# A list scheduler, token-major hash bits and DMA transposes in a masked attention with a maxout feed-forward on one core

## The chip, the cores and the metric

The kernel runs on one core of a Trainium2 chip. The metric is the device time in microseconds (us) of one execution. A run of a kernel is several executions, and its median is quoted with the lowest and the highest. An execution counts as slow when it is more than 1.5% above the fastest of the same kernel in that run; verdicts use the fast ones alone. Names of engines in profile lines: PE is TensorE's matmuls, PEld its weight loads, DVE VectorE, ACT ScalarE, POOL GpSimd, SP the engine whose queue issues most of the DMAs. "SPq" is SP's queue, "PEclk" the share of its full clock that TensorE was granted.

## The reference, cut to what matters

```python
# 4 batches, 8 heads, 768 tokens, 64 dims, 6 hash bits
q_bits = (einsum('bhsd,dk->bhsk', q, proj) > 0)       # same for k
mask   = bucket(q)[..., :, None] == bucket(k)[..., None, :]
scores = where(mask, q @ k.T / sqrt(64), -1e9)
attn   = exp(scores - max); attn = attn / (sum(attn) + 1e-9)
x      = heads side by side of (attn @ v)             # 3072 x 512
h      = maximum(maximum(x @ w1, x @ w2), x @ w3)     # 512 -> 768, three times
out    = h @ w_out                                    # 768 -> 512
```

## The kernel before

Each q and k is split into an fp16 value and its fp16 residual, side by side in 128 columns, and turned so that these 128 lie on the partitions. The hash needs all 128 rows. After it, six bit rows take the place of the first six residual rows, scaled so that a pair of different buckets gets an exponent far below zero. A score is then a matmul of 64 + 6 = 70 rows, and no mask is ever applied.

The work comes in 192 *units* (batch, half of the queries, pair of heads, head, a third of the keys). Each unit is a pair of score matmuls, one exponential over 128 x 768 on ScalarE, and six attend matmuls:

```python
def score(u):
    ...
    for i in range(2):
        nc.tensor.matmul(sc[:, i, 0:HQ], kT[0:KR, hh * NCH + 2 * j + i, :],
                         qT[0:KR, hh * NCH + hf * CH : hh * NCH + (hf + 1) * CH, :], ...)
    nc.scalar.activation(AT[:], sc[:, :, 0:HQ], ActFn.Exp, bias=bias_t[:], scale=EXP_SCALE)
```

The hash is bit-major: 32-column weights, then a comparison, then the bits are written into rows 64 to 69 of the turned operand by VectorE, or by eight small DMAs in batch 1:

```python
def hash_half(b, pr, half):
    ...
    hash_cmp(hbs[b, pr][:, half * HQ : (half + 1) * HQ], hash_mm([g]))
def hash_head_rows(b, pr, hh):
    for i, n in enumerate("qk"):
        dst = T[n, b, pr][D : D + NBITS, ...]
        hash_row(dst, hbs[b, pr][o : o + NBITS, :])
```

The normalised x is turned by TensorE before the feed-forward. The order is by hand: work is hung on unit numbers, and the feed-forward's groups of matmuls (18 of the first layer and 3 of the second for each half batch) are rationed by a credit:

```python
front(0, 1, 2); at(3, lambda: load_pair(0, 3, nc.sync)); ...
for u in range(N + LAG + 4):
    if u < N: score(u)
    if LAG <= u < N + LAG and not late: attend(u - LAG)
    for pe, fn in todo.pop(u, []): fn()
    if u >= begin:
        credit += rate
        while atoms and credit >= atoms[0][0] / 2: ...
```

The softmax here doesn't subtract the row's maximum and nothing guards it: scores larger than these inputs give would overflow.

Of the kernel before, what the change touches and what calls it, by code (L numbers as in the profile page):

```python
# [8 lines left out]
FP32 = mybir.dt.float32  # L10
# [3 lines left out]


@with_exitstack
def kernel(
# [24 lines left out]
    KR = D + NBITS  # L42

# [5 lines left out]

    konst = ctx.enter_context(tc.tile_pool(name="konst", bufs=1))  # L50
    raw = ctx.enter_context(tc.tile_pool(name="raw", bufs=4))
    spl = ctx.enter_context(tc.tile_pool(name="spl", bufs=3))
    opnd = ctx.enter_context(tc.tile_pool(name="opnd", bufs=8))
    vpool = ctx.enter_context(tc.tile_pool(name="vpool", bufs=2))
    atp = ctx.enter_context(tc.tile_pool(name="atp", bufs=4))
    small = ctx.enter_context(tc.tile_pool(name="small", bufs=4))
    xp = ctx.enter_context(tc.tile_pool(name="xp", bufs=3))
    hp = ctx.enter_context(tc.tile_pool(name="hp", bufs=12))
    op = ctx.enter_context(tc.tile_pool(name="op", bufs=4))
# [5 lines left out]


    raws = {}

    def raw_tile(n, b, pr):
        if (n, b, pr) not in raws:  # L70
            raws[n, b, pr] = raw.tile([P, 2, NCH * D], FP32, tag=n + "32", name=n + "32")
        return raws[n, b, pr]

    def load(n, b, pr, eng, heads=(0, 2)):
        h0, h1 = heads
        r_ = raw_tile(n, b, pr)
        src = {"q": q, "k": k, "v": v}[n][b, 2 * pr + h0 : 2 * pr + h1]
        eng.dma_start(r_[:, h0:h1, :], src.rearrange("h (p c) d -> p h (c d)", c=NCH))
# [3 lines left out]
    load("q", 0, 0, nc.sync, (0, 1))  # L82
    load("k", 0, 0, nc.sync, (0, 1))
    load("q", 0, 0, nc.sync, (1, 2))
    load("k", 0, 0, nc.sync, (1, 2))
    load("v", 0, 0, nc.sync)
    for n in "qkv":
        load(n, 0, 1, nc.sync)

    bias_t = konst.tile([P, 1], FP32, name="bias_t")  # L90
    nc.vector.memset(bias_t[:], EXP_BIAS)
    warm = konst.tile([P, 1], FP32, name="warm")
    nc.scalar.activation(warm[:], bias_t[:], ActFn.Exp)
    iden = konst.tile([P, P], FP16, name="iden")
    make_identity(nc, iden[:])
    ones = konst.tile([P, P], FP16, name="ones")
    nc.vector.memset(ones[:], 1.0)
    vones = []
    for i in range(2):
        t = konst.tile([P, H, NCH, D + 2], FP16, name=f"vone{i}", tag=f"vone{i}")  # L100
        nc.vector.memset(t[:, :, :, D : D + 1], 1.0)
        vones.append(t)

    ph = konst.tile([D, NBITS], FP16, name="ph")
    pr32 = konst.tile([D, NBITS], FP32, name="pr32")
    PA, PB = [], []
    for i in range(2):
        for n, l in (("PA", PA), ("PB", PB)):
            l.append(konst.tile([P, 32], FP16, name=f"{n}{i}", tag=f"{n}{i}"))
            nc.vector.memset(l[i][:], 0.0)  # L110

    def make_p(i):

        if i == 0:
            nc.vector.tensor_copy(ph[:], p32[:])
            nc.vector.tensor_tensor(out=pr32[:], in0=p32[:], in1=ph[:], op=AluOp.subtract)
        for o in (0, D):
            for l, src in ((PA, ph), (PB, pr32)):
                nc.vector.tensor_scalar(out=l[i][o : o + D, NBITS * i : NBITS * (i + 1)], in0=src[:],
                                        scalar1=1024.0, scalar2=None, op0=AluOp.mult)  # L120

    w_sb = [konst.tile([P, NJ, DF], FP16, name=f"w{i}_sb") for i in range(3)]
    wout_sb = konst.tile([P, NF, DM], FP16, name="wout_sb")

    def load_w(i, half):
        w_ap = (moe_w1, moe_w2, moe_w3)[i].rearrange("(c p) f -> p c f", p=P)
        f = slice(half * DF // 2, (half + 1) * DF // 2)
        nc.gpsimd.dma_start(w_sb[i][:, :, f], w_ap[:, :, f])


    T = {}
    S16 = {}

    def operands(b, pr):
        for n in "qk":
            S16[n, b, pr] = spl.tile([P, 2 * NCH, 2 * D], FP16, tag=n + "s", name=n + "s")
            T[n, b, pr] = opnd.tile([P, 2 * NCH, P], FP16, tag=n + "T", name=n + "T")

    def split_h(n, b, pr, eng, heads=(0, 2)):
        a = slice(heads[0] * NCH, heads[1] * NCH)  # L140
        x32 = raws[n, b, pr][:].rearrange("p h (c d) -> p (h c) d", d=D)[:, a, :]
        o = S16[n, b, pr][:, a, 0:D]
        if eng is nc.scalar:
            nc.scalar.activation(o, x32, ActFn.Copy, scale=QS)
        else:
            eng.tensor_scalar(out=o, in0=x32, scalar1=QS, scalar2=None, op0=AluOp.mult)  # L146

    def split_r(n, b, pr, heads=(0, 2)):
        a = slice(heads[0] * NCH, heads[1] * NCH)
        x32 = raws[n, b, pr][:].rearrange("p h (c d) -> p (h c) d", d=D)[:, a, :]  # L150
        s = S16[n, b, pr]
        nc.vector.scalar_tensor_tensor(out=s[:, a, D : 2 * D], in0=x32, scalar=QS,  # L152
                                       in1=s[:, a, 0:D], op0=AluOp.mult, op1=AluOp.subtract)

    def xbar(n, b, pr):
        nc.sync.dma_start_transpose(T[n, b, pr][:], S16[n, b, pr][:].rearrange("p a d -> p (a d)"))

    def pe_T(n, b, pr, hh):
        ps = mm_ps.tile([P, 512], FP32, tag="mm", name="tps")
        p16 = ps[:].bitcast(FP16)  # L160
        for c in range(NCH):
            nc.tensor.transpose(p16[:, c * P : (c + 1) * P], S16[n, b, pr][:, hh * NCH + c, :], iden[:])  # L162
        return p16

    def evac_T(p16, n, b, pr, hh, eng, c0=0, c1=NCH):
        o = T[n, b, pr][:, hh * NCH + c0 : hh * NCH + c1, :].rearrange("p a t -> p (a t)")
        if eng is nc.scalar:
            nc.scalar.copy(o, p16[:, c0 * P : c1 * P])
        else:
            nc.vector.tensor_copy(o, p16[:, c0 * P : c1 * P])  # L170

    def hash_mm(sets):

        hps = mm_ps.tile([P, 512], FP32, tag="mm", name="hps")
        ws = [(i, l[i]) for l in (PA, PB) for i in range(len(sets))]
        for m, (i, w) in enumerate(ws):
            for g, (t, hh, half) in enumerate(sets[i]):
                a = hh * NCH + half * CH
                nc.tensor.matmul(hps[32 * g : 32 * (g + 1), 0:HQ], w[:], t[:, a : a + CH, :],  # L179
                                 start=m == 0, stop=m == len(ws) - 1)  # L180
        return hps

    def hash_cmp(out, hps):
        nc.vector.tensor_scalar(out=out, in0=hps[:, 0:HQ], scalar1=0.0, scalar2=0.5,  # L184
                                op0=AluOp.is_gt, op1=AluOp.subtract)

    def hash_row(dst, src):
        nc.vector.tensor_scalar(out=dst, in0=src, scalar1=2 * BIT, scalar2=None, op0=AluOp.mult)  # L188

    hbs = {}  # L190

    def hash_pair(b, pr):
        hb = small.tile([P, HQ], FP16, tag="hb", name="hb")
        hbs[b, pr] = hb
        g = [(T[n, b, pr], hh) for hh in range(2) for n in "qk"]
        hash_cmp(hb[:], hash_mm([[(t, hh, half) for t, hh in g] for half in range(2)]))
        hash_row(hb[:], hb[:])

    def hash_half(b, pr, half):
        if half == 0:  # L200
            hbs[b, pr] = small.tile([P, S], FP16, tag="hb2", name="hb2")
        g = [(T[n, b, pr], hh, half) for hh in range(2) for n in "qk"]
        hash_cmp(hbs[b, pr][:, half * HQ : (half + 1) * HQ], hash_mm([g]))

    def hash_head_rows(b, pr, hh):
        for i, n in enumerate("qk"):
            dst = T[n, b, pr][D : D + NBITS, hh * NCH : (hh + 1) * NCH, :].rearrange("p a t -> p (a t)")
            o = 32 * (2 * hh + i)
            hash_row(dst, hbs[b, pr][o : o + NBITS, :])

    def hash_rows(b, pr):
        hb = hbs.pop((b, pr))
        for g, (n, hh) in enumerate((("q", 0), ("k", 0), ("q", 1), ("k", 1))):
            for half in range(2):
                a = hh * NCH + half * CH
                o = 32 * g + NBITS * half
                nc.sync.dma_start(T[n, b, pr][D : D + NBITS, a : a + CH, :].rearrange("p a t -> p (a t)"),
                                  hb[o : o + NBITS, :])

    def hash_head(b, pr, hh):  # L220

        tq, tk = T["q", b, pr], T["k", b, pr]
        hb = small.tile([P, HQ], FP16, tag="hb", name="hb")
        hash_cmp(hb[:], hash_mm([[(tk, hh, 0), (tq, hh, 0), (tk, hh, 1), (tq, hh, 1)]]))
        for g, (t, half) in enumerate(((tk, 0), (tq, 0), (tk, 1), (tq, 1))):
            a = hh * NCH + half * CH
            hash_row(t[D : D + NBITS, a : a + CH, :].rearrange("p a t -> p (a t)"),
                     hb[32 * g : 32 * g + NBITS, :])
# [290 lines left out]
```

## Time and profile before

| | before |
|---|---|
| time, median of 3 runs | 308.07 us (307.59 to 308.14) |
| span of the profiled execution, mean granted clock | 306.0 us, 0.974 |
| TensorE's own work, by the prediction's prices | 258 us |
| span less that work | 48 us |
| an exponential: duration, start to start | 0.90 us, 0.79 us |

The span runs from the first to the last instruction. A busy TensorE isn't one at its peak, since records of matmuls overlap (a score matmul's record lasts 332 ns in the mean, and a pair of them takes 0.33 us from start to start); the prediction explains its prices. The rows in the page's part 2 are a digit or character for each fortieth of the span (7.65 us), in tenths.

### The profile page before, as it was taken

To read this page: it belongs to the slowest core of one execution; us is meant where nothing else is said; L and a number is where in the kernel's file an instruction comes from. 1 tells how busy PE (TensorE), PEld (TensorE's weight loads), DVE (VectorE), ACT (ScalarE), POOL (GpSimd) and SP (SyncE) were. 2 spreads that over 40 slices of the span, in tenths; PEclk is the share of its full clock that TensorE was granted. 3 is DMA by queue.
4 is the path that set the end of the run, shared out by engine and by line. 5 is a ranking of instruction groups with operands and counts; after the bars stand their busy time and mean duration, and the time that the engine had idled before them with its cause. 6 is when DMAs were issued, how large, how long until landed. Compare 5 with 4: busy or idle time off the path is not lost.

```text
span 306.0 us, 7090 instructions
## 1 busy us (share of the span) xinstructions
PE 276.1 (90%) x2896; PEld 176.6 (58%) x2896; DVE 212.0 (69%) x455; ACT 200.6 (66%) x265; POOL 9.3 (3%) x17
## 2 busy tenths in 40 slices
PE   3847888989969989999999989999999999999994
PEld 1444565656646656565666556656666665666551
DVE  5687996877995867969587677969664454455551
ACT  3425658968646667777778676868676787786220
POOL 1370000000000000000000000000000000000000
PEclk9969979999997999999999999999999999999998
DMA  7999940006326285915809490926002001100202
GB/s 216 372 287 264 227 131 2 3 5 185 132 56 172 45 233 130 222 39 113 249 15 230 114 246 20 237 95 136 2 1 105 2 0 54 53 1 2 103 0 104
DMA packets 46080, 35.20 MB, mean 115 GB/s; under 512 B 26656, under 2 KB 42976, under 8 KB 46048
## 3 DMA queue, kind: packets, MB, share of 16 engines
q1 hardware_dynamic: 42016, 31.61, 37.7%
q0 software_dynamic: 3952, 3.15, 6.5%
q8 instruction: 22, 0.36, 0.5%
q14 instruction: 10, 0.08, 0.1%
q10 hardware_dynamic: 80, 0.00, 0.0%
HBM read 25.17 MB, written 6.29 MB: 103 GB/s over the span
## 4 chain that ended last, share of the span: by engine, by line
PE 74%; DVE 18%; ACT 3%; issue 2%; DMA 1%; SPq 0%; DVEq 0%; ACTq 0%
PE ps L329 28%; PE sc L265 16%; PE av L285 9%; PE po L341 9%; PE hps L179 4%; PE tps L162 4%; DVE qs L152 3%; ACT AT L269 2%; DVE hb L184 2%; DVE ks L146 2%; DVE ks L152 2%; PE xps L315 2%; DVE kT L188 2%; PE svp L244 1%; DVE t L301 1%
## 5 line engine op out<-in xcount | busy, mean ns | idle before, releaser
L269 ACT ACTIVATE AT<-sc,bias_t 128x768 f16<-128x768 f32 x192 | 169.1, 902 | 73.2 <-PE sc L265 72.7
L329 PE MATMUL ps<-xT,w_sb 128*128 128x384 f16 x576 | 112.4, 327 | 1.9 <-DVE ht L336 1.7
L265 PE MATMUL sc<-qT,kT 70*128 70x384 f16 x384 | 96.4, 332 | 4.2 <-ACT AT L269 1.6
L285 PEld LDWEIGHTS <-AT 128*128 128x128 f16 x1152 | 61.3, 98 | 31.1 <-issue 6.9
L336 DVE TENSOR_TENSOR ht<-ht,ps 128x384 f16<-128x384 f16 x96 | 52.9, 552 | 34.4 <-PE ps L329 31.6
L285 PE MATMUL av<-vone,AT 128*128 128x65 f16 x1152 | 67.1, 193 | 4.4 <-DVE t L301 4.3
L329 PEld LDWEIGHTS <-w_sb 128*128 128x128 f16 x576 | 50.8, 98 | 30.9 <-issue 5.8
L265 PEld LDWEIGHTS <-kT 70*128 70x128 f16 x384 | 34.0, 100 | 23.9 <-issue 6.4
L341 PE MATMUL po<-wout_sb,ht 128*128 128x512 f16 x144 | 34.8, 379 | 0.0
L334 ACT CAST ht<-ps 128x384 f16<-128x384 f32 x48 | 22.8, 474 | 16.3 <-PE ps L329 16.1
L301 DVE TENSOR_TENSOR t<-av,mv 128x390 f32<-128x390 f32 x32 | 17.9, 560 | 10.1 <-PE av L285 10.0
L184 DVE TENSOR_SCALAR hb<-hps 128x384 f16<-128x384 f32 x28 | 15.2, 553 | 8.7 <-PE hps L179 8.6
L162 PE MATMUL tps<-iden,qs 128*128 128x128 f16 x96 | 9.7, 259 | 12.7 <-DVE qs L152 11.9
L341 PEld LDWEIGHTS <-ht 128*128 128x128 f16 x144 | 12.8, 97 | 13.1 <-issue 0.6
L347 DVE COPY osb<-po 128x512 f32<-128x512 f32 x16 | 11.0, 688 | 11.5 <-PE po L341 11.5
L305 DVE TENSOR_TENSOR xn<-t,rr 128x384 f16<-128x384 f32 x32 | 17.9, 558 | 1.1
L152 DVE SCALAR_TENSOR_TENSOR qs<-q,qs 128x768 f16<-128x768 f32 (+1 forms) x17 | 16.5, 972 | 0.1
L162 PEld LDWEIGHTS <-qs 128*128 128x128 f16 x96 | 7.4, 116 | 14.7 <-DVE qs L152 13.3
L316 DVE COPY xT<-xps 128x384 f16<-128x384 f16 x32 | 11.3, 353 | 6.2 <-PE xps L315 5.9
L152 DVE SCALAR_TENSOR_TENSOR ks<-k,ks 128x768 f16<-128x768 f32 (+1 forms) x17 | 15.3, 906 | 0.3
L179 PE MATMUL hps<-kT,PA 128*32 128x384 f16 x64 | 11.1, 343 | 1.0 <-DVE kT L170 0.9
L170 DVE COPY kT<-tps 128x768 f16<-128x768 f16 x16 | 8.6, 553 | 4.3 <-PE tps L162 4.2
(43 smaller groups left out, 172.9 us busy)
## 6 DMA issues: line engine op xcount, KB each, us to landing
v<-in_v_dram SPq DMA_DIRECT2D x16, 384.0 KB
out_dram<-osb SPq DMA_DIRECT2D x24, 256.0 KB
q<-in_q_dram SPq DMA_DIRECT2D x15, 384.0 KB
k<-in_k_dram SPq DMA_DIRECT2D x15, 384.0 KB
w_sb<-in_moe_w_dram POOLq DMA_DIRECT2D x6, 384.0 KB, 13.3
wout_sb<-in_moe_w_out_dram POOLq DMA_DIRECT2D x1, 768.0 KB, 22.0
q<-in_q_dram SPq DMA_DIRECT2D x2, 192.0 KB
k<-in_k_dram SPq DMA_DIRECT2D x2, 192.0 KB
```

Of the source, the lines that this page charges most:

```text
L152: nc.vector.scalar_tensor_tensor(out=s[:, a, D : 2 * D], in0=x32, scalar=QS, in1=s[:, a, 0:D], op0=AluOp.mult, op1=AluOp.subtract)
L162: nc.tensor.transpose(p16[:, c * P : (c + 1) * P], S16[n, b, pr][:, hh * NCH + c, :], iden[:])
L179: nc.tensor.matmul(hps[32 * g : 32 * (g + 1), 0:HQ], w[:], t[:, a : a + CH, :], start=m == 0, stop=m == len(ws) - 1)
L184: nc.vector.tensor_scalar(out=out, in0=hps[:, 0:HQ], scalar1=0.0, scalar2=0.5, op0=AluOp.is_gt, op1=AluOp.subtract)
L265: nc.tensor.matmul(sc[:, i, 0:HQ], kT[0:KR, hh * NCH + 2 * j + i, :], qT[0:KR, hh * NCH + hf * CH : hh * NCH + (hf + 1) * CH, :], start=Tr ...
L269: nc.scalar.activation(AT[:], sc[:, :, 0:HQ], ActFn.Exp, bias=bias_t[:], scale=EXP_SCALE)
L285: nc.tensor.matmul(av[:, o : o + D + 1], AT[:, i, c * P : (c + 1) * P], vones[b % 2][:, 2 * pr + hh, 2 * j + i, 0 : D + 1], start=first, s ...
L301: nc.vector.tensor_tensor(out=t[:, :, :, 0 : D + 1], in0=av[:, :, :, 0 : D + 1], in1=mvs[b, pr][:].unsqueeze(2).to_broadcast([P, 2, CH, D ...
L329: nc.tensor.matmul(ps[:, 0:HQ], w_sb[i][:, jc, fb * P : (fb + 1) * P], xT[:, jc, :], start=jc == 0, stop=jc == NJ - 1)
L334: nc.scalar.copy(ht[:], ps[:, 0:HQ])
L336: nc.vector.tensor_tensor(out=hts[fb][:], in0=hts[fb][:], in1=ps[:, 0:HQ], op=AluOp.max)
L341: nc.tensor.matmul(ps[:], hts[fb][:, c * P : (c + 1) * P], wout_sb[:, fb, :], start=fb == 0, stop=fb == NF - 1)
```

## The change

The intent is to take work from TensorE and VectorE (transposes to DMA, the means' additions to GpSimd, a cheaper hash) and to let a program order all the engines' instructions from estimated durations, so that TensorE is filled earlier. The diff has 1,028 lines. Its core:

```diff
-    at(u + LAG + 3, lambda: x_T(b, hf, pr), 0.2)
-    ... all at(), at_end(), front(), tail(), prep() and the credit loop
+class Plan:
+    LAT = {"PE": 0.22, "DVE": 0.1, "ACT": 0.1, "POOL": 0.1, "SP": 2.0, "POOLQ": 2.0}
+    def run(self):     # greedy: each free engine takes the ready task of least priority number
+        ...
+                    if t.xfer:
+                        dma = max(dma, now + dur) + t.xfer
+                        end = dma + self.LAT[e]
# hash: a chunk of tokens is the weights, 12 columns are streamed
-                nc.tensor.matmul(hps[32 * g : 32 * (g + 1), 0:HQ], w[:], t[:, a : a + CH, :], ...)
+                    nc.tensor.matmul(hps[:, a * 2 * NBITS : (a + 1) * 2 * NBITS], T[b, pr][:, a, :], PAB[:], ...)
+        nc.vector.tensor_tensor(out=bv, in0=hv[:, :, sl, 0:NBITS], in1=neg[:, :, sl, :], op=AluOp.is_gt)
# bits: turned by TensorE, written to DRAM, read back as rows 64 to 69
+            nc.tensor.transpose(p16[0:R, n * P : (n + 1) * P], bit[:, n, :, :].rearrange(...), iden[:])
+        nc.sync.dma_start(drs[b, pr][:].rearrange("n r t -> r n t"), bts.pop((b, pr))[:])
+        nc.sync.dma_start(T[b, pr][D : D + NBITS, :, :].rearrange(...), drs.pop((b, pr))[:].rearrange(...))
# (only batch 0 pair 0 is turned a second time by TensorE, bits included, head by head)
-    blocks = [(0, hf, pr) for pr, hf in ((0, 0), (0, 1), (1, 0), ...)]
+    blocks = [(0, 0, ((0, 0), (1, 0))), (0, 0, ((0, 1), (1, 1)))]      # head 0 of both halves first
# q, k of batches 1 to 3 (of 2 and 3 already before) and x of six of the eight half batches
+        nc.sync.dma_start_transpose(operand(b, pr)[:, a0:a1, :], S16[b, pr][:, a0:a1, :]...)
+        nc.sync.dma_start_transpose(x_tile(b, hf)[:, pr, :]..., xn[:]...)
-        nc.scalar.activation(AT[:], sc[:, :, 0:HQ], ActFn.Exp, bias=bias_t[:], scale=EXP_SCALE)
+        nc.scalar.activation(AT[:], scs.pop(u)[:, :, 0:HQ], ActFn.Exp, bias=EXP_BIAS, scale=EXP_SCALE)
```

## The prediction

> **What bounds the kernel now.** I read the page's busy lines first, then stretches of time, then the groups, then the timeline and the chain at both ends. The page says that TensorE is nearly full:
>
> ```profile
> PE 276.1 (90%) x2896; PEld 176.6 (58%) x2896; DVE 212.0 (69%) x455; ACT 200.6 (66%) x265; POOL 9.3 (3%) x17
> ...
> PE   3847888989969989999999989999999999999994
> ```
>
> But busy is not dense, since matmuls overlap. So I priced each block of matmuls by the distance from its start to the start of the next block in the timeline and the chain. A score pair is 0.33 us (150.25 to 150.58), six attend matmuls 0.18 (153.54 to 153.72), four first-layer matmuls 0.65 (1.30 for eight), six second-layer ones 1.30 (3.90 for 18), one pair's hash 0.87 (16 matmuls), twelve transposes 0.67, that is 0.056 each. A 130-column mean matmul I take as a transpose too. TensorE's own work is then 192 x 0.33 = 63.4, 192 x 0.18 = 34.6, 144 x 0.65 = 93.6, 24 x 1.30 = 31.2, 16 x 0.87 = 13.9, 192 + 96 + 96 small ones x 0.056 = 21.5: **258 us**. The span is 306, so **48 us are lost**. The same prices on the instruction counts of each stretch say where: 17 us before 24 us, 5 up to 40, 14 between 40 and 100, about 6 in all between 100 and 290, 4.5 at the end. The stretches (columns: PE, PEld, DVE, ACT, POOL busy, granted clock, DMA share, GB/s):
>
> ```profile
> 16.00:24.00 8.00, 4.30 (x38) 3.63 (x39) 6.72 (x9) 1.34 (x2) 5.06 (x7) 0.57 1.21 276
> ...
> 40.00:60.00 20.00, 17.52 (x226) 12.70 (x226) 15.81 (x35) 15.26 (x19) 0.00 (x0) 0.91 0.09 28
> ...
> 150.00:200.00 50.00, 48.94 (x512) 30.58 (x511) 38.65 (x81) 36.51 (x50) 0.00 (x0) 1.00 0.66 145
> 200.00:250.00 50.00, 50.00 (x513) 31.17 (x510) 30.63 (x67) 38.03 (x51) 0.00 (x0) 1.00 0.17 49
> ```
>
> From 100 us on TensorE sets the pace and there is little left. Before that something else does: the fixed order feeds scores late, so ScalarE waits, and the feed-forward work that could fill TensorE doesn't exist until 66.9 us. In the timeline:
>
> ```profile
> 17.56 2.09 DVE L152 SCALAR_TENSOR_TENSOR qs<-q,qs 128x768 f16<-128x768 f32 x1
> ...
> 21.90 0.90 ACT L269 ACTIVATE AT<-sc,bias_t 128x768 f16<-128x768 f32 x1 [5.47 <-PE sc L265]
> ```
> ```profile
> 37.39 4.06 ACT L269 ACTIVATE AT<-sc,bias_t 128x768 f16<-128x768 f32 x5 [0.73 <-PE sc L265]
> ```
>
> VectorE reaches pair 1's split only at 16.2 us, and ScalarE starves 5.5 us. The last line gives the true price of an exponential: (4.06 - 0.90) / 4 = 0.79 us from start to start. The end is pure TensorE, then a copy and a store until 306:
>
> ```profile
> 286.24 11.37 PE ps L329 x69
> 297.62 3.90 PE po L341 x18
> 301.54 0.69 DVE osb L347
> ```
>
> [...] The first q load here is issued at 0.74 and used at 3.30[...]. [...] The split above took 2.09 us against a mean of 1.03 while GpSimd cast v and issued weights[...].
>
> **The change part by part.**
>
> *Token-major hash.* Per pair, 16 matmuls (0.87) become 24 of 12 columns, each with its own weights. By the attend rate of 0.03 each that is 0.72 (estimate), plus two bit transposes, 0.11. Over 16 pairs this is even within 1 us. VectorE loses comparison and rows (2 x 0.55 + 4 x 0.35 = 2.5 per pair) for three small operations and a copy, about 1.1 (estimate). But for every pair except batch 0's first the bits go through DRAM, two dependent DMAs.
>
> *Transposes.* Batch 1's q and k leave TensorE (96 transposes), batch 0 pair 0 gets 24 more for its second pass: 192 to 120, -4.0 us. x goes by DMA in 24 of 32 blocks (batch 0's second half too): 96 to 24, -4.0. Means: 96 matmuls to 24 + 12, -3.4, with 36 additions of v moved to GpSimd. With the hash, TensorE's work falls from 258 to about **246 us**, -12. The 32 warm-up matmuls lie in idle time.
>
> *Order.* I read it from the built program. After unit 12 TensorE holds pair 3's hash and bits before unit 13's score, and on the DMA queue the read of pair 1's bits stands behind two bit writes, the three loads of batch 1's first pair, and an x transpose which needs the norm after unit 12. Feed-forward starts near unit 36, after a 30-unit half block instead of 36. After unit 192, 72 first-layer groups and 12 second-layer groups remain, against 17 or so and 3 now.
>
> The path:
> 1. *Start to unit 13.* The inputs land no earlier, and the first scores now need bits, then a second transpose and copy, and stand behind six to eight splits and copies of 0.5 to 0.8 us on ScalarE: first exponential near 13.5 us against 9.6. Twelve exponentials (9.5) with four more copies or splits (3): unit 12 near 26. Then norm 1.9, the x transpose's issue 1.4, two bit issues 1.3, 2 us landing, while the loads (1.15 MB beside weights, some 130 GB/s, 9 us) run ahead of the bits in the same queue. So unit 13 at about **35 us**, against 31.0 now.
> 2. *Units 13 to 48*, ScalarE-bound: 36 x 0.79, seven casts or splits at 0.82 - 0.10, one copy 0.4: **34 us**, to 69.
> 3. *Units 49 to 192.* TensorE's prices on its order give 137 us, ScalarE's on its own 131. With the greater taken for each twelve units, **138**, to 207. With two score buffers and both engines 95% full I add 6% of phases 2 and 3, **10** (now 100 to 290 us loses 3% with ScalarE at three quarters). To 217.
> 4. *Tail*: 72 x 0.65 + 12 x 1.30 + 0.6 = **63**, to 280. The three evacuations per 1.95 us fit (VectorE 1.1, ScalarE 0.5).
> 5. *Last copy and store*: **4.5**. Span 284.5. The measured time exceeds the span by 2.1 now, so 286.6. [...] I round to **285**, 7.5% less.
>
> So of 23 us, 12 are work removed and 11 are idle time that the earlier filling removes, nearly all between 40 and 100 us.
>
> **Rivals.**
> *The scheduler's plan holds*: no waiting behind loads, unit 13 at 28 us, friction 3%: 285 - 7 - 5 = 273. For it: TensorE's order is dense; against: it plans 0.73 for an exponential, 0.79 here, and DMA contention isn't in it.
> *ScalarE or VectorE becomes the bound*: in-order queues arranged for durations 5 to 12% too short make each engine wait for the other. 12% friction and another 3 us at the start: 298. For it: ScalarE at 131 of 138 and VectorE near 10 of 12 us per twelve units; against: the tail of 63 us can't suffer.
> *The one DMA queue becomes the bound*: 24 transposes of q and k (1.4 to 3.3 us of issue now), 24 of x, 30 bit DMAs, in order. I count some 19 us of issue where 37 are available before unit 49, so it is hidden; if heads of the queue stall for each pair, 300 to 310.
>
> **Range and chances.** 80%: 274 to 297, from the first rival to nearly the second. Faster by over 2% means under 301.9: 0.93. Within 2%: 0.05. Slower: 0.02.
>
> **What would show it.** Right: 2,882 matmuls (2,256 of scores, attend and feed-forward, 384 hash, 30 bits, 120 + 24 transposes, 36 means, 32 warm-up); first exponential after 12 us; a hole in ScalarE between 26 and 36 us; feed-forward from about 60 us; exponentials close to 0.79 apart afterwards; about 63 us without exponentials at the end, dense. Wrong: scores waiting on bit reads at pairs of batches 1 to 3, an exponential waiting more than 1 us repeatedly after unit 48, first-layer matmuls waiting for x, or holes in the tail.

The sum comes to 284.5 us of span, and to 286.6 with the 2.1 us by which the time of before exceeds its span.

## More of the kernel before

```profile
PEclk9969979999997999999999999999999999999998
DMA  7999940006326285915809490926002001100202
DMA packets 46080, 35.20 MB, mean 115 GB/s; under 512 B 26656, under 2 KB 42976, under 8 KB 46048
```

The granted clock stays near full (0.974 in the mean) but for short dips (0.50 from about 17 to 24, 41 to 44 and 92 to 96 us), and the DMA engines are idle from about 46 to 69 us and in shorter stretches later.

## The result, and the profile after

| | time | fast executions |
|---|---|---|
| before, same session | 308.11 us (307.59 to 310.41, 4 runs) | |
| after | 294.0 us (291.31 to 298.56, 4 runs) | ratio 0.9495, 95% interval 0.9435 to 0.9556 |

Ratios are the mean time of one kernel's fast executions over that of the other's in the same rounds, so not quite the ratio of the medians. The change is 5% faster: inside the predicted range, 9 us above the predicted value.

The profile taken with this result fell on the slow execution (298.56 us, clock 0.918; the three fast ones had 0.934 to 0.942). Its page:

```profile
span 296.7 us, 7201 instructions
...
PE 270.2 (91%) x2882; PEld 178.0 (60%) x2882; DVE 178.6 (60%) x399; ACT 202.8 (68%) x291; POOL 34.3 (12%) x53
...
PE   7789149999999988997979999999999999999994
...
PEclk9699755557999999999979999999999999999999
DMA  7999999968889999999976101121001102020202
...
DMA packets 70835, 41.68 MB, mean 140 GB/s; under 512 B 51422, under 2 KB 67550, under 8 KB 70802
```

There is a hole in PE at the fifth and sixth digit (30 to 44 us), and the clock is at half from about 33 to 70 us (0.50 in every window of 1 us). Nothing like either is in the page of before. The DMA engines are busy for six tenths of the time or more in every slice up to about 160 us.

To have a fast trace, the same kernel was run again (e0 below: span 292.6 us). It shows the same two things, and it is the one read from here on. First its windows (columns as in the prediction: PE, PEld, DVE, ACT, POOL busy, granted clock, DMA share, GB/s):

```profile
28.00:40.00 12.00, 3.08 (x61) 2.44 (x59) 6.83 (x16) 4.83 (x7) 1.08 (x1) 0.75 1.22 237
40.00:60.00 20.00, 18.80 (x162) 11.95 (x163) 10.45 (x25) 14.92 (x19) 5.00 (x9) 0.50 1.09 250
...
160.00:230.00 70.00, 70.00 (x788) 46.37 (x787) 35.80 (x77) 59.38 (x82) 0.00 (x0) 1.00 0.13 38
```

The hole's cause is in the chain of waits (start, duration, what):

```profile
32.66 0.32 PE bps L298 x2
33.00 0.38 ACT bt L168
33.40 0.33 SPq L307
33.83 6.95 DMA T<-dr
40.83 0.84 PE sc L353 x2
41.75 0.82 ACT AT L359
...
44.82 0.64 PE sc L353 x2
45.46 0.33 PE av L371 x6
```

The read (`T<-dr`) is that of pair 1's bits. It takes 6.95 us, and unit 13's score can't start before it lands. The three lines before it are not pair 1's: those bits were turned at 21.92 us, and their write was issued at 23.02. What is turned (L298), copied and written (L307) from 32.66 us on are pair 3's bits. The chain passes through them because pair 1's read stands behind that write in SP's queue. Behind the hole a score pair takes 0.64 us and six attend matmuls 0.33, against 0.33 and 0.18 at full clock: the pace is 0.97 us a unit, and TensorE sets it. SP's queue shows what stands before the read:

```profile
28.67 0.31 SPq L307 DMA_DIRECT2D dr<-bt  x1
29.07 0.40 SPq L216 DMA_DIRECT2D q<-in_q_dram  x1
29.57 0.41 SPq L216 DMA_DIRECT2D k<-in_k_dram  x1
30.07 0.42 SPq L216 DMA_DIRECT2D v<-in_v_dram  x1
31.16 1.28 SPq L413 DMA_TRANSPOSE xT<-xn  x1
33.40 0.33 SPq L307 DMA_DIRECT2D dr<-bt  x1
33.83 1.70 SPq L310 DMA_DIRECT2D T<-dr  x2
```

Three loads of 384 KB and a transpose were issued in the five microseconds before it, and the DMA share is above 1. The trace also has the time at which each DMA landed. Pair 1's write had landed by 29.3 us, 4.5 us before its read was issued. The three loads landed at 36.4, 37.7 and 38.8 us, and the last of the weights, from GpSimd's queue, at 37.0. The read isn't slow by itself: the same reads of later pairs, issued at 157.93 and 162.61 us with a DMA share of 0.24 (157 to 165 us), landed in 2.2 us. How much of the 6.95 us is due to the loads and how much to the weights was not isolated.

The group of exponentials, whose counterpart in the page of before had a mean of 902 ns (L269, with the bias tile), comes out shorter. The columns are count, busy time, mean ns, and idle time before them with what ended it:

```profile
L359 ACT ACTIVATE AT<-sc 128x768 f16<-128x768 f32 x192 | 147.3, 812 | 22.1 <-PE sc L353 21.1
```

### The profile page after: what moved, and what is told of

It is laid out like the page before. It is cut to its first block, busy times and chain, and to the rows that moved or that the text cites. A ratio compares the mean times of both kernels' runs of the same rounds, so it can differ in the third digit from the quotient of the medians.

```text
span 296.7 us, 7201 instructions
## 1 busy us (share of the span) xinstructions
PE 270.2 (91%) x2882; PEld 178.0 (60%) x2882; DVE 178.6 (60%) x399; ACT 202.8 (68%) x291; POOL 34.3 (12%) x53
## 4 chain that ended last, share of the span: by engine, by line
PE 67%; DMA 13%; DVE 12%; ACT 3%; SPq 2%; issue 2%; ACTq 0%; DVEq 0%
PE ps L430 28%; PE sc L353 17%; PE av L371 10%; PE po L446 9%; DMA q<-in_q_dram 5%; DMA k<-in_k_dram 4%; DVE s L239 3%; DMA T<-dr 3%; DVE bit L286 2%; ACT AT L359 2%; DMA v<-in_v_dram 2%; PE hps L273 1%; PE tps L260 1%; DVE s L234 1%; SPq L216 1%
## 5 line engine op out<-in xcount | busy, mean ns | idle before, releaser
L359 ACT ACTIVATE AT<-sc 128x768 f16<-128x768 f32 x192 | 147.4, 812 | 22.2 <-PE sc L353 21.1
L353 PE MATMUL sc<-T 70*128 70x384 f16 x384 | 102.5, 352 | 12.7 <-DMA T<-dr 8.5
L353 PEld LDWEIGHTS <-T 70*128 70x128 f16 x384 | 31.4, 103 | 24.0 <-DMA T<-dr 8.7
L321 POOL TENSOR_TENSOR vt<-v 128x384 f32<-128x384 f32 x12 | 12.6, 1053 | 103.5 <-DMA v<-in_v_dram 103.5
L168 ACT COPY osb<-po 128x512 f32<-128x512 f32 x22 | 12.9, 586 | 17.0 <-PE po L446 16.9
L239 DVE SCALAR_TENSOR_TENSOR s<-q,s 128x384 f16<-128x384 f32 x32 | 18.5, 586 | 5.9 <-ACT s L232 5.8
L239 DVE SCALAR_TENSOR_TENSOR s<-k,s 128x384 f16<-128x384 f32 x32 | 17.5, 570 | 1.5 <-ACT s L232 1.5
L260 PE MATMUL tps<-iden,s 128*128 128x128 f16 x120 | 11.3, 251 | 3.3 <-ACT T L168 1.1
L286 DVE TENSOR_TENSOR bit<-hps,neg 128x144 f16<-128x144 f32 (+1 forms) x17 | 13.0, 764 | 0.6
L273 PE MATMUL hps<-PAB,T 128*128 128x12 f16 x384 | 12.4, 169 | 0.0
```

Source lines behind the costliest of these rows:

```text
L168: nc.scalar.copy(o, i)
L239: nc.vector.scalar_tensor_tensor(out=s[:, a0:a1, D : 2 * D], in0=raw_view(n, b, pr, heads), scalar=QS, in1=s[:, a0:a1, 0:D], op0=AluOp.mul ...
L273: nc.tensor.matmul(hps[:, a * 2 * NBITS : (a + 1) * 2 * NBITS], T[b, pr][:, a, :], PAB[:], start=True, stop=True)
L286: nc.vector.tensor_tensor(out=bv, in0=hv[:, :, sl, 0:NBITS], in1=neg[:, :, sl, :], op=AluOp.is_gt)
L353: nc.tensor.matmul(sc[:, i, 0:HQ], t[0:KR, NA2 + hh * NCH + 2 * j + i, :], t[0:KR, hh * NCH + hf * CH : hh * NCH + (hf + 1) * CH, :], star ...
L359: nc.scalar.activation(AT[:], scs.pop(u)[:, :, 0:HQ], ActFn.Exp, bias=EXP_BIAS, scale=EXP_SCALE)
```

## The experiments

All were correct, but for e4. Times are medians of four executions with the extremes; "before" is the kernel before in the same session on the same chip (e0 to e3: 307.21; e4 to e7: 308.37; e8 to e11: 309.73; seven executions each). Span less work means the profiled span less TensorE's work by price. With a pair's hash at the measured 0.60 us, the kernel after has 222.8 (scores, attend, feed-forward) + 16 x 0.60 + 210 small matmuls x 0.056 = 244 us.

| run | what | time | ratio of fast runs, 95% |
|---|---|---|---|
| e0 | after, unchanged | 295.05 (293.71 to 296.37) | 0.960 (0.954 to 0.966) |
| e1 | before, bias as a number | 308.36 (305.75 to 310.67) | 1.000 (0.993 to 1.008) |
| e2 | after, dummies in the hole | 292.98 (289.74 to 296.8) | 0.950 (0.942 to 0.958) |
| e3 | after, batch 0's bits by TensorE | 292.08 (290.41 to 293.09) | 0.949 (0.942 to 0.956) |
| e4 | e3 without 36 loads | 289.47 (287.8 to 291.48) | 0.941 (0.933 to 0.949) |
| e5 | e3, scores in order | 287.52 (284.37 to 288.26) | 0.931 (0.922 to 0.940) |
| e6 | e5, dearer DMAs in the plan | 294.96 (282.47 to 296.76) | unclear |
| e7 | e5, all x by TensorE | 290.4 (288.18 to 293.34) | 0.942 (0.933 to 0.950) |
| e8 | after, scores in order | 296.74 (294.46 to 299.6) | 0.958 (0.951 to 0.964) |
| e9 | e5, batch 1 by TensorE | 289.06 (285.95 to 291.63) | 0.928 (0.922 to 0.934) |
| e10 | e5, dummies in 110 to 125 us | 288.45 (286.21 to 290.11) | 0.933 (0.926 to 0.939) |
| e11 | e5 again | 286.64 (285.6 to 287.3) | 0.927 (0.923 to 0.931) |

The theory after reading the traces: the work fell as priced, and the idle time didn't, because of the hole and the half clock behind it. The rivals: the DMA load slows everything; the scheduler's order is at fault; the exponential's shorter form did what was gained.

### e0: the kernel after again

> The changed kernel unchanged, for a second profile (the first fell in a slow run) and as the yardstick of the runs beside it. Both theories: 291 to 295 us when fast, a hole of about 10 us without exponentials after unit 12, and a granted clock of 0.5 from the hole until some 20 to 30 us after it. If the low clock belonged only to the slow run, the profile will show 1.0 there.

295.05 us at a ratio of 0.960, against 0.9495 in the first session. The same kernel differs by 1% between the two, with granted clocks of 0.918 to 0.930 here and 0.934 to 0.942 in the fast runs there. Differences under 1% between sessions mean nothing in what follows.

### e1: the bias alone

```diff
- nc.scalar.activation(AT[:], sc[:, :, 0:HQ], ActFn.Exp, bias=bias_t[:], scale=EXP_SCALE)
+ nc.scalar.activation(AT[:], sc[:, :, 0:HQ], ActFn.Exp, bias=EXP_BIAS, scale=EXP_SCALE)
```

> The kernel before, with the exponential's bias given as a number instead of a tile, nothing else. In the changed kernel exponentials stand 0.72 us apart where they follow each other, and took 0.81, against 0.79 and 0.90 before. Theory: the bias tile cost 0.08 us, so here too 0.72 and 0.81, but the whole gains only in the ScalarE-bound part before 100 us, 1 to 3 us of 308. Rival: the 0.08 us comes from the order or the neighbours on other engines, then 0.79 stays and the time too. A part of the change that I hadn't priced.

The exponential's median fell from 900 to 811 ns, ScalarE's busy time from 200.6 to 186.7 us, and the time did not move. ScalarE waited that much more for scores (86.0 us in place of 72.7). So in the kernel before, shorter exponentials buy nothing by themselves.

### e2: keep TensorE's clock up in the hole

```diff
+    def keep_warm():
+        d = mm_ps.tile([P, 512], FP32, tag="mm", name="dps")
+        for _ in range(130):
+            nc.tensor.matmul(d[:, 0:P], ones[:], ones[:], start=True, stop=True)
+        if (b, pr) == (0, 3):
+            add(("PE", 0.0), URGENT, [bT], lambda e: keep_warm(), take=("mm",), give=("mm",))
```

> The changed kernel with 130 needless 128-column matmuls put into the hole before unit 13 (about 7.3 us of TensorE time where it idles some 8.5). Theory: the hole costs twice, once by itself and once because the clock falls to half and stays there until about 68 us, where score and attend of one unit take 0.97 us instead of 0.51. With the clock kept up units 13 to 41 follow each other by ScalarE at 0.72 plus casts, 4 to 7 us earlier; the end 3 to 6 us earlier (286 to 290). Rival: after 70 us the DMA queue sets the pace, loads of q, k and v landing late at 96 to 152 us; then what is won before 70 us is lost again and the time stays within 2 us of the changed kernel.

The fast runs had clocks of 0.965 to 0.976 (e0: 0.918 to 0.930) and a ratio of 0.950 against 0.960. The intervals overlap a little; by the two ratios it is about 1%, 3 us, the least that the theory expected, and the median of 292.98 us misses its 286 to 290. The profiled execution fell in the slow state (clock 0.948): there the dummies ended at 37.9 us, the hole went on to 40.8, and the clock fell all the same, from 42.2 to 69.5 us. So the half clock seems to cost something, which these intervals don't show firmly, and no more than a part of the missing 9 us was recovered.

### e3: no round trip through DRAM in batch 0

```diff
-        if heads == (0, 2):
+        if heads == (0, 2) and not direct:
...
+        if by_pe:
+            hb = add(("DVE", 0.85), p0 + 5, [hm], lambda e: hash_bits(b, pr, (0, 2), e, True), give=("mm",))
+            for hh in range(2):
+                for n in "qk":
+                    t = add(("PE", 0.34), p0 + 6, [hb], lambda e, n=n, hh=hh: pe_T(n, b, pr, hh, e), take=("mm",))
+                    ready_T[b, pr, hh].append(add(both(0.5, 0.72), p0 + 7, [t], lambda e, ...: evac_T(n, b, pr, hh, e), ...))
+            return
```

> The changed kernel with the bits of batch 0's pairs 1 to 3 sent through a second TensorE transpose, as pair 0's are, instead of through DRAM: no dependent DMA pair in the start. The scheduler orders everything anew. Theory: unit 13 no longer waits for the bit read behind three loads; its score comes by 33 us instead of 41, the clock stays up, and the end moves by 8 to 14 us, to 279 to 286. Rival (DMA queue sets the pace later): the first 60 us gain as much, but less than 4 us arrive at the end.

A miss: 292.08, only 3 us better than e0, at the price of 66 more small matmuls (3.7 us of work). The hole is gone: the time lost by price in 28 to 41 us fell from 10.5 to 1.8 us. But the half clock came back elsewhere. The clock row of its page:

```profile
PEclk9799999999999999755999999999999999999999
```

And the timeline of TensorE just there (start, duration, engine, line, operation, count, and in brackets the idle time before it with its releaser):

```profile
116.80 0.48 PE L353 MATMUL sc<-T 70*128 70x384 f16 x2 [0.96 <-ACT AT L359]
...
119.85 0.30 PE L298 MATMUL bps<-iden,bit 128*72 128x128 f16 x2 [0.75 <-DVE bit L292]
...
121.38 0.80 PE L353 MATMUL sc<-T 70*128 70x384 f16 x2 [0.63 <-ACT AT L359]
```

No long wait precedes the drop. There is a thin stretch, in which TensorE waits up to a microsecond at a time for ScalarE and VectorE and little feed-forward is left to fill it; the last score pair above already takes 0.80 us. Lost by price: 5.2 us in 100 to 120, 8.6 in 120 to 140. By span less work: 292.6 - 244 = 48 in e0, 290.8 - 248 = 43 in e3.

### e4: e3 without the loads of batches 1 to 3

```diff
     def load(n, b, pr, heads, e):
+        if b > 0:
+            raws[n, b, pr] = raws[n, 0, pr]
+            return
```

The results are wrong: batches 1 to 3 work on batch 0's data, in the order of e3.

> Wrong results on purpose. The kernel with batch 0's bits by TensorE (e3_bits_pe), every compute instruction in the same order, but batches 1 to 3 have no loads of q, k and v: they work on batch 0's tiles again. 14 MB less DMA, the transposes, bits and stores stay. e3 still loses some 24 us of TensorE between 28 and 140 us. Theory: these are DMA, loads and transposes sharing one queue that can't keep up, and engines whose fixed order stands behind a split that waits for them. Then most of it goes: 273 to 279 us. Rival: it is the coupling of TensorE, ScalarE and VectorE in fixed orders made from wrong durations; then without loads it stays above 287.

Another miss of its theory: the time stays above 287 us, as the rival in the text has it. A third of the traffic is gone (27.3 MB in place of 41.5), the time is 0.8% below e3's by ratio, which between sessions means nothing, and the clock drops at the same place:

```profile
PEclk9598999999999999755999999999999999999999
DMA  6999501945787764396851113001130002020202
```

The loads are not what thins that stretch. The DMA transposes remained in this kernel, and were tried in e9.

### e5: scores in order

```diff
-    s = add(("PE", 0.33), u, ready_T[b, pr, hh], lambda e, u=u: score(u, e), ...)
+    s = prev_s = add(("PE", 0.33), u, ready_T[b, pr, hh] + [prev_s], lambda e, u=u: score(u, e), ...)
```

> e3_bits_pe with one more dependence in the scheduler: each score after the one before it. In the changed kernel the scheduler let later blocks' scores go ahead while a pair wasn't ready. Nothing is done less; 121 instead of 82 first-layer groups stand before the last score. Also the control for the two runs after it. If the DMA queue sets the pace up to 140 us, feed-forward placed elsewhere fills little before that: within 3 us of e3. If it is a lack of feed-forward work between the scores, 4 to 8 us faster than e3.

287.52 us, ratio 0.931 against e3's 0.949, and the intervals do not touch, though the two are of different sessions and chips. In e3 the plan lets later blocks' scores run ahead; ordered, more feed-forward groups come before the last score (121 in place of 82 first-layer groups). Its rows of PE and clock, and windows of a microsecond around what is left of the drop:

```profile
PE   7789999997989997799998999999999999999994
...
PEclk9689999999999999959999999999999999999999
```
```profile
120.00:121.00 1.00, 0.30 (x2) 0.18 (x3) 0.14 (x1) 0.79 (x2) 0.00 (x0) 1.00 0.82 93
121.00:122.00 1.00, 0.20 (x1) 0.10 (x1) 0.92 (x2) 1.00 (x3) 0.00 (x0) 0.83 0.95 356
122.00:123.00 1.00, 1.00 (x9) 0.63 (x8) 0.96 (x4) 0.75 (x2) 0.00 (x0) 0.50 0.92 279
```

The drop lasts some 7 us here, against 17 in e3.

### e6: tell the plan what DMAs cost

```diff
-  ... load(...), xfer=1.1   -  ... xbar(...), xfer=2.1   -  ... x_bar(...), xfer=0.6
+  ... load(...), xfer=1.4   +  ... xbar(...), xfer=3     +  ... x_bar(...), xfer=0.9
```

> e5_scores_in_order, and the scheduler told that transfers take longer: 3.0 instead of 2.1 us for a transpose of q or k, 0.9 instead of 0.6 for x, 1.4 instead of 1.1 for a load. Same work, same DMA. Theory (orders stand behind transfers that the plan took for landed): 3 to 8 us faster than e5, the waits on DMA at splits become fewer. Rival (the queue is full, whatever the order): within 2 us of e5.

No verdict: one execution took 282.47 us at a mean clock of 0.997, the other three 293.62 to 296.76 at 0.931 to 0.946. By the definition above the three count as slow, so nothing rests on them. As an observation: in one program with one order, executions with a fallen clock were 11 to 14 us longer. The profiled one had it at half for four to five slices:

```profile
PEclk9899999999999985555999999999999999999999
```

### e7: all x by TensorE

```diff
-            if (b, hf) in ((0, 0), (B - 1, 1)):
+            if True:
```

> e5_scores_in_order with every x transposed on TensorE again: one of the change's parts undone. TensorE +4.0 us (72 transposes x 0.056), VectorE and ScalarE 24 copies of 0.36 more, DMA 24 transposes less. If the DMA queue is the bound up to 140 us, its relief is worth more than the 4 us: 2 to 6 us faster than e5. If TensorE is the bound: 3 to 4 us slower than e5, the part pays.

290.4 us, ratio 0.942 against e5's 0.931 in the same session: about 3 us slower, for 72 small matmuls more, 4.0 us of work by price. On these medians x by DMA pays about the work that it takes away; the two intervals just overlap.

### e8: scores in order, with the bits still through DRAM

The one line of e5, in the kernel after.

> The kernel after with one edit: each pair of score matmuls waits in the scheduler for the pair before it, as in e5, while the hash bits of batch 0's pairs 1 to 3 keep their round trip through DRAM. If order alone is worth what it brought on top of e3 (292.08 to 287.52, 4.6 us), this runs at about 290.5 (288 to 293). If the hole at 28 to 41 us and the half clock behind it decide, whatever the order, it stays at 294 to 296, the time of the kernel after, and the clock of 0.5 shows again at about 35 to 65 us.

296.74 us, ratio 0.958 against e0's 0.960: order alone is worth nothing. The score still waits for the bits, now in one piece, and the half clock follows:

```profile
39.63 1.46 PE L353 MATMUL sc<-T 70*128 70x384 f16 x4 [9.19 <-DMA T<-dr]
```
```profile
PE   7798059999999999969979999999999999999994
...
PEclk9799555559999999999979999999999999999999
```

So with the four combinations: neither edit 0.960, order alone 0.958, bits alone 0.949, both 0.931 and 0.927. They are of three sessions, but order alone and both together (e8 and e11) stood side by side in one. The order pays only once the hole is closed.

### e9: batch 1 by TensorE too

```diff
-        by_pe = b == 0
+        by_pe = b <= 1
```

> e5 with batch 1's q, k and bits turned by TensorE as batch 0's are, 184 more small matmuls at 0.056 us = 10.3 us of TensorE work, and no DMA transposes of q and k before batch 2. If these DMA transposes hold up the stretch of 80 to 140 us, its 10.8 us of lost time by price (2.2, 3.3 and 5.3 us per 20 us slice) falls to about 3 and the clock stays at 1.0 there: 286 to 290, with the clock above 0.985. If that stretch is thin for another reason (the in-order ScalarE waiting for a load, the small matmuls themselves), the 10 us are simply added in part: 291 to 297.

289.06 us; its two fast executions give a ratio of 0.928, e11 has 0.927 beside it. The profile fell on a slow execution (290.57 us, 0.3 us over the limit, at a clock of 0.988; the fast ones had 0.991 and 0.999). As far as one such profile shows it, the first theory holds in the mechanism. The time lost by price in 80 to 140 us is 3.3 us against 8.7 in e11, and the clock stays up:

```profile
PEclk9989999999999999999989999999999999999999
```

But the stretch is filled by the 10.3 us of transposes that the DMA engines did before, and the total doesn't move. The DMA transposes of batch 1 save TensorE work, and in a stretch where it then idles.

### e10: dummies in the thin stretch

```diff
+        for _ in range(6 if 72 <= u < 82 else 0):
+            nc.tensor.matmul(sc[:, 0, 0:P], ones[:], ones[:], start=True, stop=True)
```

> e5 with six dummy matmuls of 128 columns ahead of each of the ten scores 72 to 81 (about 3.4 us of TensorE work at full clock, in the stretch of 110 to 125 us). If a clock that falls behind thin stretches is what is left to win, the clock stays above 0.985 and the time falls to 284 to 287. If the dummies only take room, 288 to 291.

288.45 us, clocks 0.975 to 0.988 (e11: 0.976 to 0.982), a ratio of 0.933 against 0.927: no gain. The dummies took about their room, or slightly less, and did not raise the mean clock. In the profiled execution the clock did stay at 1.00 from 100 to 140 us, but it was at half from 47.2 to 50.6 and from 67.7 to 71.1 us, where e11's wasn't. One profile of each doesn't tell whether the dummies or chance moved the dip.

### e11: the best version again

> The kernel of e5 unchanged, on the chip of these runs, to compare e8, e9 and e10 with: 287.5 (284 to 291), ratio to the kernel before 0.931 (0.92 to 0.945).

286.64 us, ratio 0.927. With e5's 0.931 it is the fastest kernel that ran steadily, some 3% under the kernel after (0.960) and 7% under the one before. e6's single 282.47 at a clock of 0.997 suggests that an order which never lets the clock fall would bring more; one execution doesn't show it.

## Why the prediction was right or wrong

The direction, the class and the range were right, and the value of 285 was 9 us low. That it came so near is partly luck: steps 1 and 2 were 13 us late together, and step 3 was 4 us early, which the prediction didn't foresee. Step by step, with e0's fast trace:

| step of the prediction | predicted | e0 |
|---|---|---|
| 1. start to unit 13 | 35 us | 41.75 (+6.75) |
| 2. units 13 to 48, to the 49th exponential | 34, to 69 us | 40.5, to 82.26 (+6.5) |
| 3. units 49 to 192 | 148, to 217 us | 144.0, to 226.3 (-4) |
| 4. tail | 63 us | 62.3 |
| 5. last copy and store | 4.5 us | 4.0 |
| span | 284.5 us | 292.6 |

**Work removed: right.** 2,882 matmuls as counted. The hash of 24 small matmuls takes 0.58 to 0.60 us, a little less than the estimated 0.72, so TensorE's work is 244 us, not 246. The tail is dense and as long as priced; it lay beyond the reach of every wait.

**Idle time: the step that failed.** The prediction has "11 are idle time that the earlier filling removes, nearly all between 40 and 100 us". Span less work is 292.6 - 244 = 48 us, just what it was before. It lies elsewhere: the hole of 28 to 41 us loses 10.5 us by price, 41 to 70 us loses 12.6; of the rest the start has most (12.5), then 96 to 160 us (6.2) and the end (4). These add up to some 3 us less than 48, since an instruction across a border counts in both windows and a hash matmul was priced at 0.028 us there. In before these were 5 (24 to 40 us) and 14 (40 to 100 us).

**Step 1, mechanism right, size off.** The bits behind two bit writes, three loads and an x transpose in one queue: that is what the trace shows. The sum allowed "2 us landing" for the read, and it took 6.95 us with the DMA engines full (a share of 1.22 in 28 to 40 us); the 2 us are what a read takes when they are not (2.2 at 157.93 us), and about what the first q load of before took from the end of its issue to its use (1.15 to 3.30 us). The sum's rate for the three loads, "some 130 GB/s", was near: in e0 the last landed 9.7 us after the first was issued, about 120 GB/s (an estimate from 3 x 384 KB and these times). The first exponential came at 15.46 us, not 13.5. Between it and unit 13 another term was under-counted in a visible way: VectorE's share of a pair's hash was put at "about 1.1 (estimate)", which agrees with three small operations and a copy in the trace of before (0.19, 0.26, 0.29 and 0.35 us: lines L304, L188, L247 and L316), and the comparison of 128 x 144 elements alone takes 0.81 us (line L286, three times on the chain before the hole, from 20.84 us on).

**Step 2, mechanism wrong.** "Units 13 to 48, ScalarE-bound: 36 x 0.79". Up to 66.6 us TensorE sets the pace at half clock, 0.64 + 0.33 = 0.97 us a unit with hash, bits and x transposes in between, and the half clock came with the hole of step 1: in e3, without the hole, the clock is full from 15 to 120 us, and in e8, with it, at half from 30 to 67. The prediction read the clock of 0.57 in the 16 to 24 us of before, and added a hole of its own at 26 to 35 us, but never asked what clock TensorE would have after it. That the clock matters for the time is what e2 points to (about 3 us when it stays up, by intervals that overlap a little); in e6 the clock and the time went together.

**Step 3, a little too dear.** 144.0 in place of 148. The exponentials follow each other at 0.72 us (three in 2.25), not at 0.79, since the bias is now a number (e1: 900 to 811 ns by this edit alone); the prediction carried over the old spacing and missed that the diff changes the operand. How much of the 4 us is due to this was not isolated; e1 shows that it is worth nothing in the kernel before. One reading of the prediction was off without weight here: the first feed-forward group of before starts at 63.90 us, not at 66.9.

**The rivals.** "The one DMA queue becomes the bound" came true once, for 7.9 us at pair 1 (one wait in the whole trace), and for no pair of batches 1 to 3. That the loads of the later batches are not what holds up the later stretch is shown by e4; the DMA transposes stayed in it. "In-order queues arranged for durations too short" is nearest to what e3 found: thin stretches in which TensorE waits for ScalarE and VectorE, and then the clock. What the scheduler itself contributes is shown by e5 and e8: scores that overtake each other cost nothing with the hole in place and about 2% once it is closed.

**Where the hoped-for gain went.** Removing the hole (e3) brought 3 us net, since the extra TensorE work and the next thin stretch took the rest. Closing both (e5, e11) leaves about 286.5 - 248 = 39 us and 284.8 - 248 = 37 us of span less work: the 11 us of idle time that the prediction expected were to be had, by these two edits. What is not settled: why the stretch of 100 to 140 us is thin. e4 rules out the loads, e9 shows that it fills up when batch 1's transposes are on TensorE, but this adds work as well as removing transfers, so it does not tell a late transfer from a mere lack of TensorE work.

## What to carry to other kernels

Price a hole twice: once for its length and once for the clock with which TensorE comes out of it (in e0, 10.5 us lost by price in 28 to 41 us, and 12.6 in 41 to 70 us, where the clock was 0.50 up to 68). Work moved from TensorE to the DMA engines pays where TensorE is the bound (x here, about 3 us by intervals that just overlap) and not where it then waits (q and k of batch 1: with them on TensorE again a ratio of 0.928, against 0.927); and a small transfer that a whole engine waits for doesn't belong in a queue behind bulk loads (6.95 us, against 2.2). In a list scheduler, check that a free choice of order doesn't spend the filler early, and compare several runs with their clocks before believing a few per cent.

## What the runs measured of the hardware

- TensorE's clock behind a hole: in e0 it stayed at 0.50 from 34 to 68 us, though TensorE's records are busy for 18.80 of the 20 us in 40 to 60; it came back at 68.1, after the first feed-forward groups (from 66.57). Scores of 70 rows and attend matmuls of 65 columns, with a few small ones between them, did not bring it back there. What it takes to bring it back, no run here isolates.
- TensorE's clock in a thin stretch: in e5 it fell at about 121.7 us with no single wait above 1.30 us in the 20 us before (the last two, 0.43 and 1.30 us, had two small transposes between them). In windows of 1 us of before and after only two levels occur, 1.00 and 0.50, with other values only where a window spans a change.
- A small transfer behind bulk ones: in e0 the read of the bits (36 KB) took 6.95 us with three 384 KB loads ahead of it, and 2.2 us where the DMA share was 0.24.
- An exponential's bias: given as a tile, 900 ns for 128 x 768 (before, the median); given as a number, 811 (e1). The prediction missed it.
- VectorE's comparison of 128 x 144 elements, with a strided 16-bit result: 802 ns in the mean of 15 (after). Whether the stride is the reason was not tested.
